# Batch 0's v loaded in two halves of heads, the second among the first weight slices, and the opening's scores, transposes and values in another order

## Chip, cores and metric

One core of a Trainium2 chip. The metric is the device time of one execution in microseconds; a profile's span, which is shown too, is some 2 us shorter. The four runs of the kernel before lie within 0.88 us, 0.24%. Times of "the kernel before" beside an experiment come from the same chip and rounds.

## The reference

Causal attention over 8 batches of 8 heads, with 16 beacon keys that every query sees, followed by a gated feed-forward block over all 4,608 tokens:

```python
B, H, S, Nb, D = 8, 8, 576, 16, 64
k_all = concat([beacon_k, k], axis=2); v_all = concat([beacon_v, v], axis=2)
scores = q @ k_all.T / sqrt(D)            # causal mask on the 576 own keys
attn = softmax(scores) @ v_all            # (B, H, S, D)
x = attn.transpose(0, 2, 1, 3).reshape(B * S, H * D)        # (4608, 512)
out = (gelu(x @ w_gate) * (x @ w_val)) @ w_out              # d_ff = 1536
```

Inputs and outputs are float32 in HBM; the kernel computes in bf16, and the loads convert.

## The kernel before

Heads are worked in four pairs (`m`). `transpose_both(0, m)` turns q and k of a pair on TensorE. `scores(0, (m, c))`, here `c((m, c))`, computes one of four chunks of a pair's scores and its exponential. `av` multiplies a pair's exponentials with v and normalises; `av_head` does one head. `turn` and `put` transpose the result into the feed-forward's input. Batch 0 has nothing to overlap with: it is the opening, and the dense gate/value matmuls (`gv_mms`) begin at its end.

```python
psum_s = ctx.enter_context(tc.tile_pool(name="psum_s", bufs=3, space=bass.MemoryType.PSUM))
psum_t = ctx.enter_context(tc.tile_pool(name="psum_t", bufs=1, space=bass.MemoryType.PSUM))
psum_o = ctx.enter_context(tc.tile_pool(name="psum_o", bufs=1, space=bass.MemoryType.PSUM))
# ... cut
def key_loads(src, beacon, dst, b):        # five loads, one for each tile of up to 128 keys
    parts = [(dst[NB:P, 0, :, :], src[b, :, 0:112, :].rearrange("h p d -> p h d"))]
    # ... cut: beacon
    for j in range(1, 5):
        n = KROWS[j]
        r0 = 112 + (j - 1) * P
        parts.append((dst[0:n, j, :, :], src[b, :, r0 : r0 + n, :].rearrange("h p d -> p h d")))
    return [lambda o=o, i=i: dma(o, i) for o, i in parts]      # dma: issued by GpSimd
# ... cut
def attend(b, m, hi, x_ps):                # 15 matmuls of one head
    expT, v_sb = exp_ring[:, m, :, :], v_ring[b % NRING]
    for j in range(5):
        for t in range(j + 1):
            e0 = EXP_OFF[t] + (j - t) * P
            mm(x_ps[:, j * DV : (j + 1) * DV], expT[0 : KROWS[t], hi, e0 : e0 + P],
               v_sb[0 : KROWS[t], t, 2 * m + hi, 0:DV], t == 0, t == j, skip_group_check=True)
# ... cut: the loads of the opening; load_qk6(b, h0, h1) loads k, then q of heads h0 to h1
load_qk6(0, 2, 4, (0,))
load_qk6(0, 4, 6)
load_qk6(0, 6, H)
for load in key_loads(v, beacon_v, v_ring[0][:, :, :, 0:D], 0)[1:]:
    load()
load_gate_val(0, 2)
load_gate_val(2, 4)
load_gate_val(4, 8)
# ... cut: the compute, see the diff
turn(0, 0); put(0, 0, by_act=True)
turn(0, 1, psum_o, "o"); put(0, 1, by_act=True)
av(0, 3)
gv_mms(0, 0, 0)
turn(0, 2); put(0, 2, by_act=True)
gv_mms(0, 1, 0)
turn(0, 3, psum_o, "o"); put(0, 3)
```

The softmax here doesn't subtract the row's maximum and nothing guards it: scores larger than these inputs give would overflow.

## Time and profile before

| | before |
|---|---|
| median of 4 runs | 366.34 us (365.75 to 366.63) |
| span of the profile, mean granted clock | 364.4 us, 0.999 |
| TensorE busy | 354.3 us, 97% |
| last y transposes of batch 0 end, dense stretch begins | 24.02 us |
| last load of v lands / last of four 256 KB weight slices lands | 16.34 / 21.62 us |

The first 24 us are the only place that the change touches; most of the page is shown in the prediction. One more view belongs here, the waits of TensorE from 7 to 34 us (who waited for whom: total, times, longest):

```profile
PE s_ps L168 <- DVE qkT L217: 1.3, 3, 0.5
PE s_ps L168 <- ACT qkT L171: 0.7, 1, 0.7
PE t_ps L176 <- DMA qk<-in_q_dram: 0.6, 1, 0.6
PE s_ps L168 <- issue: 0.2, 1, 0.2
```

In sum 2.8 us, in pieces of at most 0.7: this is what a better order could win, and it also tells that TensorE never stood for long.

### The profile page before, as it was taken

How to read it: one execution, taken by the hardware profiler on the slowest of the kernel's cores; microseconds unless marked ns; L12 is line 12 of the kernel's file. 1: busy time of each engine (PE TensorE's matmuls, PEld its weight loads, DVE VectorE, ACT ScalarE, POOL GpSimd, SP SyncE). 2: the span in 40 equal slices, each digit the busy share in tenths (PEclk: the TensorE clock that was granted, in tenths of full speed). 3: DMA queues.
4: the chain of work that ended last, by engine and by line, in shares of the span. 5: the costliest groups of instructions: out<-in, count | busy, mean ns of one | idle time of the engine just before them, and what ended most of it. 6: DMA issues, size and time to landing. Idle time of an engine off the chain costs nothing.

```text
span 364.4 us, 7627 instructions
## 1 busy us (share of the span) xinstructions
PE 354.3 (97%) x3127; PEld 184.6 (51%) x3170; DVE 155.4 (43%) x305; ACT 189.0 (52%) x243; POOL 161.2 (44%) x288
## 2 busy tenths in 40 slices
PE   7899999999999999999999999999999999999996
PEld 6664446444654456445644464446544564444443
DVE  4546545433454335343533354434444353333332
ACT  3973489136933594339723892379335953321210
POOL 8934388565537452954475554646330530000000
PEclk9999999999999999999999999999999999999999
DMA  7999999799069995999299927991697033000103
GB/s 103 175 203 204 197 124 91 125 187 186 20 121 126 199 87 65 171 216 64 57 146 208 126 35 120 178 197 24 108 142 132 17 64 114 0 0 31 58 34 112
DMA packets 160419, 41.57 MB, mean 114 GB/s; under 512 B 146944, under 2 KB 155904, under 8 KB 160384
## 3 DMA queue, kind: packets, MB, share of 16 engines
q0 software_dynamic: 104848, 19.11, 69.5%
q1 hardware_dynamic: 55536, 21.96, 29.3%
q8 instruction: 25, 0.41, 0.5%
q14 instruction: 10, 0.08, 0.1%
HBM read 38.27 MB, written 9.44 MB: 131 GB/s over the span
## 4 chain that ended last, share of the span: by engine, by line
PE 94%; issue 1%; DMA 1%; DVE 1%; POOL 1%; POOLq 0%; DVEq 0%
PE gv_ps L168 48%; PE o_ps L168 25%; PE x_ps L168 9%; PE s_ps L168 8%; PE v_ps L168 2%; PE g_ps L168 2%; DMA qk<-in_q_dram 1%; PE t_ps L176 1%; DVE qkT L213 1%; POOL qk L111 0%; PE y_ps L176 0%; DVE hT_sb L426 0%; POOL eye L480 0%; DVE o_sb L445 0%; DVE qkT L217 0%
## 5 line engine op out<-in xcount | busy, mean ns | idle before, releaser
L171 ACT ACTIVATE ge_sb<-gv_ps 128x512 bf16<-128x512 f32 x101 | 59.4, 597 | 142.8 <-PE gv_ps L168 140.6
L426 DVE TENSOR_TENSOR hT_sb<-gv_ps,ge_sb 128x512 bf16<-128x512 f32 x101 | 69.0, 691 | 113.5 <-ACT ge_sb L171 111.1
L168 PE MATMUL gv_ps<-xT_sb,wg_sb 128*128 128x512 bf16 x402 | 111.4, 379 | 0.5
L168 PE MATMUL gv_ps<-xT_sb,wv_sb 128*128 128x512 bf16 x388 | 107.9, 379 | 0.4
L171 ACT ACTIVATE expT<-s_ps 128x992 bf16<-128x992 f32 (+3 forms) x112 | 100.6, 974 | 6.5 <-PE s_ps L168 5.4
L168 PE MATMUL o_ps<-wo_sb,hT_sb 128*128 128x512 bf16 (+2 forms) x420 | 99.9, 373 | 2.0 <-issue 0.9
L298 POOL TENSOR_SCALAR_AFFINE_SELECT expT<-expT 128x256 bf16<-128x256 bf16 (+1 forms) x140 | 52.3, 390 | 52.9 <-ACT expT L171 51.8
L168 PEld LDWEIGHTS <-wv_sb 128*128 128x128 bf16 x432 | 42.3, 98 | 50.6
L168 PEld LDWEIGHTS <-wg_sb 128*128 128x128 bf16 x432 | 42.0, 98 | 50.0
L168 PEld LDWEIGHTS <-hT_sb 128*128 128x128 bf16 x444 | 39.9, 98 | 41.7 <-issue 1.7
L168 PEld LDWEIGHTS <-expT 128*128 128x128 bf16 (+1 forms) x960 | 33.6, 97 | 9.8 <-DVE y_sb L334 2.9
L445 DVE COPY o_sb<-o_ps 128x512 f32<-128x512 f32 (+2 forms) x37 | 24.9, 672 | 31.2 <-PE o_ps L168 30.2
L168 PE MATMUL x_ps<-v_sb,expT 128*128 128x65 bf16 (+1 forms) x960 | 37.4, 193 | 0.0
L111 POOL DMA_DIRECT2D v_sb<-in_v_dram x40 | 33.6, 857 | 5.9 <-DMA wv_sb<-in_moe_w_val_dram 1.7
L168 PE MATMUL s_ps<-qkT 64*128 64x80 bf16 (+5 forms) x528 | 33.1, 250 | 2.3 <-DVE qkT L217 1.3
L111 POOL DMA_DIRECT2D k_sb<-in_k_dram x30 | 25.2, 842 | 14.7 <-DMA q_sb<-in_q_dram 11.3
L334 DVE TENSOR_TENSOR y_sb<-x_ps,r_sb 128x320 bf16<-128x320 f32 (+1 forms) x47 | 28.8, 612 | 1.6
L111 POOL DMA_DIRECT2D q_sb<-in_q_dram x30 | 25.3, 874 | 5.2 <-DMA wo_sb<-in_moe_w_out_dram 3.6
L332 DVE RECIPROCAL r_sb<-x_ps 128x5 f32<-128x5 f32 (+1 forms) x47 | 9.6, 204 | 42.3 <-PE x_ps L168 42.3
L168 PEld LDWEIGHTS <-qkT 64*128 64x128 bf16 x528 | 17.1, 95 | 17.8 <-issue 12.9
L377 POOL COPY hold_sb<-xT_sb 128x2 bf16<-128x2 bf16 x6 | 1.1, 186 | 31.1 <-DMA xT_sb<-y_sb 31.1
L111 POOL DMA_DIRECT2D k_sb<-in_beacon_k_dram x6 | 3.2, 534 | 13.4 <-DMA v_sb<-in_v_dram 13.4
(54 smaller groups left out, 123.3 us busy)
## 6 DMA issues: line engine op xcount, KB each, us to landing
out_dram<-o_sb SPq DMA_DIRECT2D x35, 256.0 KB, 7.0
v_sb<-in_v_dram POOLq DMA_DIRECT2D x24, 128.0 KB, 9.1
q_sb<-in_q_dram POOLq DMA_DIRECT2D x18, 128.0 KB, 11.8
k_sb<-in_k_dram POOLq DMA_DIRECT2D x18, 128.0 KB, 5.9
wo_sb<-in_moe_w_out_dram POOLq DMA_DIRECT2D x3, 512.0 KB, 14.4
wg_sb<-in_moe_w_gate_dram POOLq DMA_DIRECT2D x2, 512.0 KB, 11.4
wv_sb<-in_moe_w_val_dram POOLq DMA_DIRECT2D x2, 512.0 KB, 13.0
v_sb<-in_v_dram POOLq DMA_DIRECT2D x8, 112.0 KB, 5.4
```

The lines of the kernel that those rows point to most:

```text
L111: keep(nc.gpsimd.dma_start(out=out_ap, in_=in_ap))
L168: keep(nc.tensor.matmul(out_ap, lhsT, rhs, start=start, stop=stop, **kw))
L171: keep(nc.scalar.activation(out_ap, in_ap, func, **kw))
L176: keep(nc.tensor.transpose(out_ap, in_ap, ident[0:n, 0:n]))
L213: keep(nc.vector.tensor_copy(out_ap, in_ap))
L298: nc.gpsimd.affine_select(out=d, in_=d, pattern=[[0, 2], [1, n]], compare_op=ALU.is_ge, fill=0.0, base=0, channel_multiplier=-1,)
L332: keep(nc.vector.reciprocal(r, x[:, :, :, D:DV]))
L334: nc.vector.tensor_tensor(out=y_of[i][:, :, h0:h1, :].rearrange("p j b d -> p b j d"), in0=x[:, :, :, 0:D], in1=r.to_broadcast([P, h1 - h0 ...
L377: keep(nc.gpsimd.tensor_copy(hold_sb, x[:, 0 : S : S - 1]))
L426: nc.vector.tensor_tensor(out=h_of[ci][:, fi, :], in0=gv_of.pop((ci, fi))[1], in1=ge_sb, op=ALU.mult)
L445: keep(nc.vector.tensor_copy(o_sb[:, ti, c0:c1], o_ps))
```

## The change

Its intent: v of heads 0 to 3 arrives before q and k of the last pair, so that the first pair's values can fill TensorE's idle time. They now stand right behind chunk (2,1), the heads of pairs 1 and 2 stand singly between the last chunks, and the transposes of pairs 1 and 3 come one chunk later. The other half of v shares the queue with the weights that the gate/value matmuls want. The diff in full:

```diff
--- before.py
+++ after.py
@@ -153,9 +153,13 @@
         for load in key_loads(v, beacon_v, v_ring[b % NRING][:, :, :, 0:D], b):
             load()
 
-    def load_gate_val(f0, f1):
+    def v_half(h0):
+        hs = slice(h0, h0 + 4)
+        return key_loads(v[:, hs], None, v_ring[0][:, :, hs, 0:D], 0)
+
+    def load_gate_val(f0, f1, ws=(0, 1)):
         fs = slice(f0 * P, f1 * P)
-        for w in range(2):
+        for w in ws:
             dma(
                 (wg_sb, wv_sb)[w][:, :, fs],
                 (moe_w_gate, moe_w_val)[w][:, fs].rearrange("(kk p) f -> p kk f", p=P),
@@ -489,11 +493,14 @@
     )
     load_qk6(0, 2, 4, (0,))
     load_qk6(0, 4, 6)
+    for load in v_half(0):
+        load()
     load_qk6(0, 6, H)
-    for load in key_loads(v, beacon_v, v_ring[0][:, :, :, 0:D], 0)[1:]:
+    first = [lambda f0=f0, w=w: load_gate_val(f0, f0 + 2, (w,)) for f0 in (0, 2) for w in (0, 1)]
+    for load in v_half(4):
         load()
-    load_gate_val(0, 2)
-    load_gate_val(2, 4)
+        if first:
+            first.pop(0)()
     load_gate_val(4, 8)
     load_qk6(1, 0, 4)
     load_kb(1)
@@ -521,25 +528,26 @@
     transpose_both(0, 0)
     c((0, 0))
     c((0, 2))
+    c((0, 1))
     transpose_both(0, 1)
-    c((0, 1))
     c((1, 0))
     c((1, 2))
     transpose_both(0, 2)
     c((0, 3), (1, 3))
     c((1, 1))
     c((2, 0))
+    c((2, 2))
     transpose_both(0, 3)
-    c((2, 2))
     c((2, 1))
+    av(0, 0)
     c((3, 0))
+    av_head(0, 1, 0, psum_t, "t")
+    c((2, 3), (3, 3))
+    av_head(0, 1, 1, psum_o, "o")
     c((3, 2))
-    av_head(0, 0, 0, psum_t, "t")
-    av_head(0, 0, 1, psum_o, "o")
-    c((2, 3), (3, 3))
-    av(0, 1)
+    av_head(0, 2, 0, psum_t, "t")
     c((3, 1))
-    av(0, 2)
+    av_head(0, 2, 1, psum_o, "o")
     turn(0, 0)
     put(0, 0, by_act=True)
     turn(0, 1, psum_o, "o")
```

## The prediction

> **What bounds the kernel now.** I read the page first, then the chain of waits up to 30 us, then the engines one by one in the first 30 us, and last the DMA issues in short windows.
>
> ```profile
> PE 354.3 (97%) x3127; PEld 184.6 (51%) x3170; DVE 155.4 (43%) x305; ACT 189.0 (52%) x243; POOL 161.2 (44%) x288
> PE 94%; issue 1%; DMA 1%; DVE 1%; POOL 1%; POOLq 0%; DVEq 0%
> ```
>
> TensorE is busy for 354.3 of 364.4 us and makes up 94% of the chain that ended last. After the opening there is no wait of note on it, so whatever moves the start of the dense gate/value matmuls of chunk 0 moves the end by as much. The change touches only what lies before them. In the record before, the last of batch 0's four y transposes begins at 23.75 us and the dense stretch at 24.02 us: I take 24.02 as the mark.
>
> ```profile
> 14.21 1.42 DVE qkT L213 x2
> 15.63 0.08 DVE qkT L217
> 15.72 0.05 issue
> 15.76 0.90 PE s_ps L168 x12
> 16.66 1.02 PE x_ps L168 x30
> ...
> 23.27 0.43 PE gv_ps L168 x2
> 23.71 0.05 issue
> 23.75 0.43 PE y_ps L176 x5
> ```
>
> This is the chain in order of time (start, length, what). Up to 15.76 it hops between transposes and their copies; from 15.76 to 24 it is TensorE in program order, with a pause of 0.20 at 19.43 ("issue") and about 0.2 ahead of the last transposes. Beside it ScalarE does the exponentials:
>
> ```profile
> 9.96 9.59 ACT L171 ACTIVATE expT<-s_ps 128x992 bf16<-128x992 f32 x11 [0.46 <-PE s_ps L168]
> 20.16 1.00 ACT L171 ACTIVATE expT<-s_ps 128x992 bf16<-128x992 f32 x1 [0.60 <-PE s_ps L168]
> ```
>
> Eleven in a row without a gap, 9.59 / 11 = 0.87 us each, a gap of 0.46 before them and of 0.60 before the last. These two gaps and TensorE's idle time before 15.76 are what the reordering aims at. Now the loads:
>
> ```profile
> 7.00 4.20 POOL L111 DMA_DIRECT2D v_sb<-in_v_dram  x5
> 15.95 0.68 POOL L111 DMA_DIRECT2D qk<-in_k_dram  x1 [0.24 <-DMA v_sb<-in_v_dram]
> 19.59 0.76 POOL L111 DMA_DIRECT2D wg_sb<-in_moe_w_gate_dram  x1 [1.65 <-DMA wv_sb<-in_moe_w_val_dram]
> v_sb<-in_v_dram POOLq DMA_DIRECT2D x1, 80.0 KB, 5.9
> wv_sb<-in_moe_w_val_dram POOLq DMA_DIRECT2D x1, 256.0 KB, 8.3
> kb<-in_beacon_k_dram POOLq DMA_DIRECT2D x1, 16.0 KB, 12.4
> 12.00:14.00 2.00, 1.60 (x45) 1.17 (x45) 1.15 (x3) 2.00 (x3) 2.00 (x3) 1.00 2.42 154
> 18.00:20.00 2.00, 1.80 (x50) 1.43 (x44) 1.35 (x4) 1.55 (x2) 0.41 (x1) 1.00 1.45 195
> ```
>
> Three lines are issues, three are issues with their time to landing, two are windows with DMA share and GB/s at the end. Issue start plus time to landing: the last tile of v is issued at 10.35 and lands at 16.25, just ahead of the first values matmul (16.59); the last of the four small weight slices is issued at 13.36 and lands at 21.66. Sixteen KB of beacon keys need 12.4 us, so the loads queue behind one another and size hardly matters. v moves at 154 GB/s, the weights at 195 to 207. From about 3 us the DMA engines never rest here: the transfers are the limit, not the issuing.
>
> [...] landings follow issue order, and the 12.4 us of the beacon keys are the wait for what stood ahead. [...] The trace has the clock at 1.00 throughout, with pauses of 0.7 us at most[...].
>
> **The change part by part.**
>
> *Loads.* Five loads of v (576 KB) become ten of half the heads. Bytes are the same. An issue of a full tile takes about 0.85 us, that of the 80-row one 0.77, of the 16 KB beacon 0.53: as an estimate from these, 0.65 for a half. The order becomes q and k up to the third pair, first half of v (288 KB), q and k of the fourth pair, then half tile, gate slice, half tile, value slice, and so on, the fifth half tile last. In the trace before, q of the third pair lands at 5.13 + 5.5 = 10.6 us and from there the queue drains continuously:
> - first half of v: 288 KB (0.295 MB) at 154 GB/s = 1.9, lands by 12.5;
> - q and k of the fourth pair: 288 KB in the 1.6 us of before (10.6 to 12.2) or a little more, 14.2 (before 12.2);
> - second half of v, 1.9, and four slices of 256 KB (1.05 MB) at 200 GB/s, 5.2: together 7.1, so the last half tile lands near 21.4; the half tiles one by one near 14.6, 16.4, 18.0, 19.7, 21.4.
>
> The sum is a cross-check: the same bytes ended at 21.66 before, with a weight slice last. Issuing: ten times 0.65, six of 0.63 and 0.80 put the last half tile's issue end near 17, so it isn't what is late. (Some issues also start about 0.3 us after the landing of the load eight places earlier: 15.95 after 15.6, 19.59 after 19.3. With that the estimate is still 17.)
>
> *Scores and transposes up to 16 us.* The third chunk of pair 0 no longer sits behind the transposes that wait for q until 8.96; ScalarE runs three exponentials from 7.65 to 10.4 and pauses 0.4 for the keys of pair 1, as before 0.46. Gain about 0.1, for eleven exponentials then follow at 0.87 from 10.8. The fourth pair's transposes come at 13.9 and finish when q lands, 14.75; their copies (1.42 + 0.16) end at 15.85. Before: 15.71. The chunk of pair 3 isn't needed before 16.1, so this delay is hidden.
>
> *First values pair.* It runs at 15.15 to 16.2, as soon as the exponential of chunk (2,0) frees its PSUM tile, in what was idle time; all it reads landed at 12.5. That takes 1 us out of the stretch after 15.76. With everything on time I follow: (3,0) 16.2, half of pair 1 16.55, (2,3)+(3,3) 17.1, other half 17.5, (3,2) 18.0, first head of pair 2 at 18.4.
>
> *The new wait.* That head is head 4, in the second half of v. Its fifteen matmuls (0.51 us) go through the key tiles; the last five need the fifth half tile, 21.4. So TensorE stands in parts from about 18.7 to 21.45, and, since it runs in program order, chunk (3,1) stands behind it. From there:
> - last matmuls to 21.7, chunk (3,1) 0.4 to 22.1, its exponential 22.2 to 23.15;
> - other head of pair 2 to 22.6, its normalisation 0.7 to 23.4 (it holds the tile that the turn of pair 1 wants), turn of pair 0 beside it, turn of pair 1 at 23.45 to 23.7;
> - values of pair 3, 0.95, 24.65; gate/value 0.43, turn 0.26, gate/value 0.43 give 25.8;
> - normalisation of pair 3 (0.22 + 0.82) is ready at 25.75; last turn 0.27: dense start near 26.05.
>
> Against 24.02 that is 2.0 us later. Without the new wait the same walk gives (3,1) at 18.9 to 19.3, and, with the turn of pair 1 waiting 0.4 for its tile, a dense start near 23.4 to 23.7: 0.3 to 0.6 earlier. So reordering +0.4 gain, loads −2.4 net of it.
>
> **The rivals.**
> 1. *v is in time after all*: 365.9. For it: [...] the author will have wanted it. Against: order in the queue, and 1 MB of weights that must pass first. It would have to come 2 us sooner.
> 2. *GpSimd's issuing becomes the bound*: if a half costs as much as a full tile, five more issues add at most 5 x 0.85 = 4.2 us up to the last small slice: 14.2 + 4.2 = 18.4, still before 21.4. Time as in the main case. Later weights (slices of features 4 to 8) landed at 24.2 and 26.7 before and are first read at 30.07, a slack of 3 us; the shift of the dense start widens it.
> 3. *The clock falls in the stall*: two pauses of about 1.0 and 1.5 us, broken by five matmuls[...].
> 4. *The stall is absorbed later*: TensorE shows only 0.05 us pauses in the chain from 24 to 45 us, so there is nothing to absorb it.
>
> **Range and chances.** 366.33 + 2.0, less a little because I may have put the last half tile too late (at 20.9 the loss is 1.5), makes 368.2. Rival 1 stretches the low end to about 366.3 and rival 3 with a late queue the high end to 369.3. Two per cent are 7.3 us, out of reach of anything found here; the verdict "same" is nearly sure.
>
> **What would show it.** Right: in the trace after, the values matmuls of head 4 idle before a DMA of v for over 1 us in all between 18 and 22; the last half tile lands at 20.8 to 21.8; the exponential of (3,1) starts after 21.5 (20.16 before); the first values matmul is at about 15.2; the dense start is at 25.5 to 26.2. Wrong: head 4 runs without a wait, or the last v lands before 19; then the time falls to about 366. If the loss is there but the values wait for nothing, another wait has taken its place and my reading of the loads failed.

Rival 3 was priced near 370 us. The forecast's sum came to a dense start near 26.05, 2.0 us after 24.02, and to 366.33 + 2.0, less a little, so 368.2 us. The high end of the range, 369.3, leaned on rival 3; it was the author's estimate. Two exceptions to "1.00 throughout" and "0.7 us at most": the trace of before has a clock of 0.50 in the last 0.6 us of its span, after TensorE's work, and a pause of 1.1 us ahead of the first warm-up matmul.

## The result

The changed kernel takes **371.81 us** (371.50 to 372.86, 4 runs) against 366.34 us. A ratio here is the mean time of one kernel's fast runs over that of the other's of the same rounds, so not quite the ratio of these medians: 1.0156, interval 1.0131 to 1.0181. That is 1.6% slower; the prediction had 368.2, with a range of 366.3 to 369.3. Span 370.2 us.

The page's busy time of TensorE and the clock in 40 slices of 9.3 us, changed kernel:

```profile
PE 360.6 (97%) x3170; PEld 187.4 (51%) x3170; DVE 155.6 (42%) x307; ACT 189.5 (51%) x243; POOL 164.2 (44%) x293
...
PEclk9869999999999999999999999999999999999999
```

The second and third slices have a lower clock (0.8 and 0.6 in whole tenths). TensorE is even busier than before (354.3): at the lower clock matmuls were busy for longer (thirty values matmuls 1.65 us against 1.02, below), so busy time hides this loss. The chain of work that ended last, 16 to 34 us, changed kernel (start, length, what):

```profile
17.08 6.19 DMA v_sb<-in_v_dram
23.27 0.04 issue
23.31 0.22 PE x_ps L172
23.53 0.81 PE s_ps L172 x9
24.33 0.95 PE x_ps L172 x15
...
26.09 0.67 PE y_ps L180 x5
26.76 1.65 PE x_ps L172 x30
```

The chain no longer starts from a transpose's copy but from the last half tile of v, issued at 17.08 and landed at 23.27 (before 17.08, outside this view, it runs through GpSimd's issues from 11.23 on). Behind it come, in program order, one matmul of head 4, the chunk (3,1) and the rest. Thirty values matmuls take 1.65 us; in the chain of before they took 1.02. The dense stretch begins at 29.99 us, 5.97 after the 24.02 of before; the span grew by 5.8. All of the loss is in the opening.

TensorE's longest wait from 7 to 34 us, and stretches with TensorE's busy time (second pair of numbers: us busy, instructions) and, third from the end, the granted clock:

```profile
PE x_ps L172 <- DMA v_sb<-in_v_dram: 3.1, 2, 1.8
...
12.00:15.30 3.30, 3.30 (x57) 2.36 (x55) 1.15 (x4) 3.30 (x5) 3.30 (x5) 0.50 1.27 143
...
18.80:22.20 3.40, 1.37 (x30) 0.95 (x27) 0.74 (x3) 1.58 (x2) 2.65 (x5) 1.00 1.55 175
22.40:28.90 6.50, 5.27 (x72) 4.28 (x72) 1.78 (x6) 2.30 (x3) 2.46 (x5) 0.50 1.26 203
```

The clock fell twice, to 0.50: from 11.93 to 15.34 us and from 22.17 to 29.00 us, by the clock records of the trace. The second fall lies exactly on the path from v's landing to the dense stretch. The GpSimd queue shows how the loads were issued (start, us, what; in brackets the idle time before):

```profile
5.75 3.62 POOL L111 DMA_DIRECT2D v_sb<-in_v_dram  x5
...
11.23 0.72 POOL L111 DMA_DIRECT2D v_sb<-in_v_dram  x1 [0.61 <-DMA qk<-in_q_dram]
...
17.08 0.71 POOL L111 DMA_DIRECT2D v_sb<-in_v_dram  x1
```

A half tile costs 0.72 us to issue on average over the five, hardly less than the 0.84 of a full one.

### The profile page after: what moved, and what is told of

Same layout as the page of the kernel before. It is cut to its first block, busy times and chain, and to the rows that moved or that the text cites. A ratio compares the mean times of both kernels' runs of the same rounds, so it can differ in the third digit from the quotient of the medians.

```text
span 370.2 us, 7677 instructions
## 1 busy us (share of the span) xinstructions
PE 360.6 (97%) x3170; PEld 187.4 (51%) x3170; DVE 155.6 (42%) x307; ACT 189.5 (51%) x243; POOL 164.2 (44%) x293
## 4 chain that ended last, share of the span: by engine, by line
PE 93%; DMA 3%; POOL 2%; issue 0%; DVE 0%; POOLq 0%
PE gv_ps L172 47%; PE o_ps L172 26%; PE x_ps L172 8%; PE s_ps L172 7%; DMA v_sb<-in_v_dram 2%; PE v_ps L172 2%; PE g_ps L172 2%; DMA qk<-in_q_dram 2%; PE t_ps L180 1%; POOL v_sb L111 1%; POOL qk L111 1%; POOL wg_sb L111 0%; POOL wv_sb L111 0%; PE y_ps L180 0%; DVE y_sb L338 0%
## 5 line engine op out<-in xcount | busy, mean ns | idle before, releaser
L172 PE MATMUL gv_ps<-xT_sb,wv_sb 128*128 128x512 bf16 x404 | 111.7, 379 | 0.0
L172 PE MATMUL o_ps<-wo_sb,hT_sb 128*128 128x512 bf16 (+2 forms) x444 | 104.7, 373 | 0.0
L172 PE MATMUL x_ps<-v_sb,expT 128*128 128x65 bf16 (+1 forms) x960 | 39.3, 196 | 3.2 <-DMA v_sb<-in_v_dram 3.1
L172 PEld LDWEIGHTS <-expT 128*128 128x128 bf16 (+1 forms) x960 | 34.9, 99 | 11.9 <-issue 3.4
L111 POOL DMA_DIRECT2D v_sb<-in_v_dram x45 | 36.8, 834 | 7.0 <-DMA wv_sb<-in_moe_w_val_dram 1.9
L172 PE MATMUL s_ps<-qkT 64*128 64x80 bf16 (+6 forms) x528 | 33.8, 255 | 1.8 <-DVE qkT L221 1.0
L172 PEld LDWEIGHTS <-qkT 64*128 64x128 bf16 x528 | 17.2, 96 | 18.5 <-issue 14.2
```

The source lines that it names most:

```text
L111: keep(nc.gpsimd.dma_start(out=out_ap, in_=in_ap))
L172: keep(nc.tensor.matmul(out_ap, lhsT, rhs, start=start, stop=stop, **kw))
```

## The experiments

My theory after the result: the loads did it, through a v that lands at 23.3 instead of 21.4 us and through the clock that falls in the wait. Rivals: the new order itself; the clock as a mere symptom. Eleven runs of ten different kernels follow. Some of their diffs are abridged, and the labels are not quite in order.

### e1: the new order with the old loads

```diff
 # changed kernel with the loads of before
-    for load in v_half(0): load()
     load_qk6(0, 6, H)
-    # second half one by one with the weight slices
+    for load in key_loads(v, beacon_v, v_ring[0][:, :, :, 0:D], 0)[1:]: load()
+    load_gate_val(0, 2); load_gate_val(2, 4)
```

> The new order of the compute with the old loads. My theory (the loss of 5.5 us comes from the loads: v's second half lands at 23.3 us behind 1 MB of weights, and the tensor clock falls while TensorE waits for it): no wait for v beyond about 16.3 us, no fall of the clock after 20 us, dense gate/value stretch near 24.2 us, time 366.5 (365.8 to 367.2). The first fall of the clock (12 to 15.3 us) should still be there if the third chunk of pair 0 ahead of the transposes causes it. Rival (the order itself is the loss: a head of pair 2 ahead of the last chunk, and single PSUM tiles that make turn wait for normalisation): 369 or more.

Measured: 367.07 us, ratio 1.0027 (1.0012 to 1.0042); dense stretch at 24.75 us in its profile; clock 0.995 to 1.0 in five runs. No wait for v is shown. TensorE's waits, 7 to 34 us as before:

```profile
PE s_ps L172 <- DVE qkT L221: 1.5, 2, 1.1
PE s_ps L172 <- ACT qkT L175: 0.7, 1, 0.7
PE y_ps L180 <- DVE y_sb L338: 0.6, 1, 0.6
```

They sum to 2.8 us again. The 0.6 for q and the 0.5s for keys became one piece of 1.1, and the turn of pair 1 now waits for the normalisation that holds its PSUM tile. So the order isn't the loss of 5.5 us, but it isn't a gain either: it costs about 1 us where I had credited 0.4. The first fall of the clock, which I had expected in this run, wasn't there in the profile.

### e2: the new loads with the old order

```diff
 # before's sequence of transpose_both, c, av, av_head; the changed kernel's loads
```

> The new loads with the old order of the compute. My theory: v's last half tile lands near 23.3 us as in the changed kernel; the values of pair 2 wait for it, but the last chunk and its exponential are done by then, so the dense stretch begins at 26.5 us if the clock holds and near 28.5 if it falls: 368.8 to 370.8. No fall of the clock at 12 us, since the third chunk of pair 0 stands behind the transposes again. Rival (the order is the loss): 366 to 367.

Measured: 370.23 us, ratio 1.0114 (1.0098 to 1.0130), as the theory said. Values of pair 2 wait 2.7 us for v, the last half tile's matmul starts at 23.27, the clock is at half from about 24.2 to 27.6 us (means of 0.54 and 0.60 over 24 to 26 and 26 to 28), dense stretch at 28.17. The rival is out: the loads alone give 4.2 us of the loss. Loads and order added (4.2 + 1.0) are about the whole (5.7 by the ratio).

### e3: both halves of v ahead of the weights

```diff
-    first = [lambda f0=f0, w=w: load_gate_val(f0, f0 + 2, (w,)) for f0 in (0, 2) for w in (0, 1)]
     for load in v_half(4):
         load()
-        if first:
-            first.pop(0)()
+    load_gate_val(0, 2)
+    load_gate_val(2, 4)
```

> As the changed kernel, but the five loads of v's second half stand together ahead of the weight slices. My theory: they land by 16.5 us, head 4 waits for nothing, the last small slice lands near 21.5 (22.95 in the changed kernel), dense stretch near 24.0 us, time 366.2 (365.6 to 367.0). If the interleaving itself costs DMA time (half tiles between slices took 0.8 us each instead of 0.4), the 4 slices and 5 half tiles here take 7.1 us and not 9.0. Rival (ten small loads are slow wherever they stand): last slice at 23 us, values late, 368 or more.

Measured: 368.06 us, ratio 1.0068 (1.0044 to 1.0093), 367.5 to 370.3, with the higher times in the runs of lower clock (0.991, 370.3; 1.0, 367.5). Head 4 waits for nothing, as expected. But the other expectations missed, the time (365.6 to 367.0) among them: v's last load landed near 17.6 us, and the last small slice at 16.58 + 7.9 = 24.5 us, later still than in the changed kernel. And the span grew by 2.0 us although the dense stretch began at 24.98, only 0.96 later than before. The rest is lost just before 55.5 us: TensorE waits 1.2 us for a causal mask on GpSimd. e10 takes up both points.

### e4: the wait filled with dummy matmuls

```diff
     for j in range(5):
+        for _ in range(fill[j]):     # (0, 0, 0, 50, 40), head 4 only
+            mm(x_ps[:, 384:448], idle[:, 0:P], idle[:, 0:D], True, True, skip_group_check=True)
         for t in range(j + 1):
```

> The changed kernel with 50 and 40 matmuls of zeros (64 columns, into unused columns of the same PSUM tile) ahead of the last two key tiles of head 4, that is in the wait for v. My theory: v still lands at 23.3 us, but the clock stays at 1.00 after 20 us, and the work from there to the dense stretch takes about 4.7 us (6.7 in the changed kernel): dense stretch near 28.0, time 369.8 (369.3 to 370.4), so 1.6 to 2.2 us below the changed kernel. Rival (the clock is a symptom and costs nothing on the path): 371.5 to 372.

Measured: 373.13 us, ratio 1.0185 (1.0164 to 1.0207): no gain over the changed kernel, its median even 1.3 us higher. The clock was still full near 26.7 us (five y transposes from 26.33 on took 0.42 us, as in the kernel before; 0.67 at half clock in the changed one), but with the added instructions came a wait of another kind. TensorE in order of time, and the instruction queue from 23.8 to 26.3 us:

```profile
26.23 0.27 PE L172 MATMUL x_ps<-v_sb,expT 128*128 128x65 bf16 x3 [1.82 <-issue]
```

```profile
q8 instruction: 1, 0.02, 2.4%
```

In the middle of a head TensorE stood 1.82 us for no data, while one block of instructions came in. That the block was what it stood for is not shown: such a block comes in near this time in other kernels too (at 22.15 us in the changed one) without a wait of this kind. The test of the clock is void; it was made again with the number of instructions unchanged.

### e6: the wait filled, the number of instructions kept

```diff
-    warm(66)      # 64 columns each
+    warm(33)      # 128 columns each
+        # ahead of key tiles 3 and 4 of head 4: 18 and 15 matmuls of zeros
+        mm(x_ps[:, 328:512], idle[:, 0:P], idle[:, 0:184], True, True, skip_group_check=True)
```

> The filling of the wait once more, this time with 18 and 15 matmuls of zeros of 184 columns, and with 33 warm-up matmuls of 128 columns in place of 66 of 64, so that TensorE has as many instructions as in the changed kernel. In the first try the clock held up to 27 us [...]. Theory (the clock's fall costs about 2 us of the path): [...] the clock stays at 1.00 from 16 us on, v lands near 23.2, dense stretch near 28.0, time 369.8 (369.3 to 370.4). [...] Rival (the clock costs nothing on the path): 371.5 or more [...].

Measured: 370.23 us, ratio 1.0115 (1.0095 to 1.0134), against 1.0156 of the changed kernel. The same two stretches in this kernel:

```profile
18.80:22.20 3.40, 2.86 (x51) 2.54 (x48) 0.86 (x3) 1.71 (x2) 2.26 (x5) 1.00 1.61 179
22.40:28.90 6.50, 5.87 (x103) 4.37 (x101) 2.80 (x7) 3.47 (x5) 2.61 (x4) 1.00 1.27 205
```

The clock stays at 1.00, and v's last matmuls still end near 23.6 us. The dense stretch begins at 28.31 us instead of 29.99. So useless work, put where TensorE waits anyway, wins back about 1.5 us of time: the second fall of the clock is a cause on the path. The late v and the order are the rest: with the clock held the time is still 4.2 us above the kernel before. The first fall (12.04 to 15.45 us) was in this run too, so it isn't what costs.

### e5: the last chunk ahead of head 4

```diff
     c((3, 2))
+    c((3, 1))
     av_head(0, 2, 0, psum_t, "t")
-    c((3, 1))
```

> The changed kernel with chunk (3,1) put ahead of head 4, so that it no longer stands behind the wait for v. Theory (program order behind the late v costs the chunk's own time, some 0.8 us at half clock; the rest of the loss is v and the clock): dense stretch near 29.2 us, time 371.0 (370.5 to 371.4), 0.5 to 1.0 below the changed kernel. Rival (the chunk and its exponential behind the wait are the main part): 369.5 or less. [...]

Measured: 371.61 us, ratio 1.0152 (1.0135 to 1.0169): the gain that I expected is barely there. Dense stretch at 29.63. There was no first fall of the clock in this profile (1.00 from 8 to 22 us), and that changed nothing either. Program order behind the late v is a small term; v and the second fall stay.

### e7: the weight slices ahead of v's second half

```diff
     load_qk6(0, 6, H)
+    load_gate_val(0, 2)
+    load_gate_val(2, 4)
     for load in v_half(4):
         load()
-        if first:
-            first.pop(0)()
```

> As the changed kernel, with the four weight slices ahead of the five loads of v's second half. Theory (the changed kernel's DMA queue runs low between 10 and 15 us, because half tiles of 64 KB are issued at 0.72 us each, 91 GB/s, and GpSimd waits 0.6 us for a landing; large slices issued first keep it full): the last half tile lands at 21.3 to 21.9 and not at 23.3, although it stands last here too; dense stretch 26.5 if the clock holds, up to 28.3 if it falls, time 368.6 to 370.6. Rival (v's second half is slow to move wherever it stands): lands at 23 or later, time 371.5 or more.

Measured: 371.43 us, ratio 1.0151. The last half tile landed at 17.4 + 5.6 = 23.0 us. This expectation failed: large loads in front didn't make the nine loads quicker (23.27 in the changed kernel). Either mixing or the small loads themselves had to be the cause, which the next two runs separate. This trace already tells something, in two windows (GB/s at the end of the line):

```profile
13.00:14.00 1.00, 0.61 (x14) 0.35 (x10) 0.41 (x2) 1.00 (x3) 1.00 (x3) 1.00 0.51 61
20.00:21.00 1.00, 0.00 (x0) 0.00 (x0) 0.00 (x0) 0.05 (x1) 0.75 (x1) 1.00 2.26 154
```

The queue had already run low at 13 to 14 us, behind the first five half tiles: the first slice was issued only at 11.57 us, after GpSimd had stood 0.95 us for the landing of a q. The second five half tiles, with a full queue ahead of them, then moved at 154 GB/s, as full tiles did before. So half tiles were not slow to move here; what they did is let the queue run low.

### e9 and e11: full tiles mixed with weight slices

```diff
 # order of compute: before
     load_qk6(0, 6, H)
-    for load in key_loads(v, beacon_v, v_ring[0][:, :, :, 0:D], 0)[1:]: load()
-    load_gate_val(0, 2); load_gate_val(2, 4)
+    # tile 0 of v (all heads), gate slice, tile 1, value slice, tile 2, gate slice, ...
```

> Old order of the compute; the five full tiles of v stand behind q and k of the fourth pair, one by one with the four weight slices. It asks why the loads of the changed kernel moved only 2.89 MB by 22 us (3.28 MB before). If mixing v with weights slows the queue, the DMA rate between 13 and 20 us is near 150 GB/s here too and about 2.9 MB are moved by 22 us; if the small loads of half the heads are the cause, it is near 185 and 3.2 MB or more. Either way the first values wait for the last tile at 21.4 to 23 us, so the time is long: 370 to 373.

Three runs took 372.4 us, one 939 us, and the profile was of that one, with TensorE's weight loads waiting for "issue" throughout (574 us in all); why, I don't know. It is left out of the ratio (1.0173). The kernel was run again for a profile:

> The kernel of the full tiles mixed with weight slices, once more and for its profile alone, because the profile of the first time fell into a run of 939 us. Expected if full tiles mixed with weights don't slow the queue, as that profile's first 22 us say: 3.2 to 3.3 MB moved by 22 us, v's last tile at 21.3 us, values of pair 0 waiting for it, 372.4 us. If the slow state falsified those first 22 us: about 2.9 MB and v's last tile at 23.

It took 372.54 us (one run, so of unknown state), and v's last tile landed at 22.2 us. The stretch from 14 to 22 us, GB/s at the end of the line, of the kernel before, the changed one and this one:

```profile
14.00:22.00 8.00, 7.34 (x192) 6.13 (x189) 4.61 (x11) 7.11 (x10) 5.12 (x9) 1.00 1.50 196
```

```profile
14.00:22.00 8.00, 6.17 (x143) 4.89 (x140) 3.82 (x9) 5.93 (x7) 7.25 (x12) 0.92 1.47 158
```

```profile
14.00:22.00 8.00, 3.12 (x61) 2.09 (x60) 1.50 (x3) 4.74 (x6) 5.27 (x9) 0.82 1.71 187
```

Adding up 1 us windows from 2 us on, the kernel before had moved 3.28 MB by 22 us, this one 3.26 MB, the changed one 2.89 MB. Mixing full tiles with weights cost nothing in rate here. (Its values, which now need all of v, wait for it 4.7 us; hence the long time.)

### e10: half tiles where the full ones stood

```diff
 # kernel before, order of compute and of loads unchanged
     load_qk6(0, 6, H)
-    for load in key_loads(v, beacon_v, v_ring[0][:, :, :, 0:D], 0)[1:]:
-        load()
+    for pair in zip(v_half(0), v_half(4)):
+        for load in pair: load()
```

> Old order of the compute and old order of the loads, but each of the five loads of v in two halves of four heads, one behind the other. If small loads are the cause of the lost DMA rate (GpSimd issues one in 0.72 us, so 64 KB come at 91 GB/s), v's last load lands at 17.4 to 18 us (16.25 before), 3.0 MB or less are moved by 22 us, and the values of pair 0 wait about 1 us: 366.8 to 367.6. If mixing is the cause, v lands by 16.8, 3.2 MB or more by 22 us, and the time is 366.0 to 366.6.

Measured: 369.21 us, ratio 1.0074 (1.0054 to 1.0094), 2.79 MB by 22 us. Windows from 14 to 17 us, before and in this kernel:

```profile
14.00:17.00 3.00, 2.54 (x62) 1.81 (x59) 1.50 (x3) 3.00 (x5) 2.70 (x5) 1.00 1.71 186
```

```profile
14.00:17.00 3.00, 2.54 (x68) 1.94 (x65) 1.40 (x5) 3.00 (x4) 3.00 (x5) 1.00 1.27 88
```

The small loads are the cause of the lost rate: ten issues of 0.72 us bring at most 64 KB each, 91 GB/s, less than the queue drains (154 for v); the time from issue to landing shrinks from 5.3 to 2.7 us from the first half tile to the last, a queue running empty, and the rate drops to 88 GB/s. v itself landed at 16.3 us, in time; my figure of 17.4 missed, since the last issues meet an empty queue. Where are the 2.7 us lost then? TensorE's waits from 48 to 60 us:

```profile
PE x_ps L172 <- POOL expT L302: 1.8, 2, 1.7
```

The late weights hold GpSimd: its later loads wait for landings, the last four loads of q for batch 2 are issued from 48.4 us (45.8 before), and the causal masks of batch 1 stand behind them in its program. In that wait the clock falls again (mean 0.61 from 56 to 60 us). It is the 1.2 us of e3. The changed kernel shows no such wait; there TensorE comes to batch 1 some 6 us later.

A caution on marks from single profiles: the dense stretch of this run began at 22.82 us, 1.2 earlier than in the profile of the kernel before, with the same order of compute. The q of the second pair had landed at 8.20 us instead of 8.96 (e8: 8.01, dense stretch at 23.32). So such marks differ by about a microsecond through one early load alone; the ratios over several runs are the firmer evidence.

### e8: an attempt at a better kernel

```diff
 # kernel before
     c((2, 3), (3, 3))
-    av(0, 1)
     c((3, 1))
+    av(0, 1)
     av(0, 2)
```

> The kernel before, loads and order, with only the chunk (3,1) ahead of the values of pair 1. It is meant as a version better than both: ScalarE's gap of 0.6 us before the last exponential should close. Expected: last exponential starts at 19.6 us (20.16 before), dense stretch near 23.7 us (24.02), time 365.9 (365.6 to 366.3), 0.3 below the kernel before. Rival (TensorE in program order is the limit there, so that nothing is won): 366.1 to 366.4.

Measured: 365.98 us against 366.03 of the kernel before, ratio 1.0000 (0.9985 to 1.0015). ScalarE's gap is closed (before: 11 exponentials in a row, then a gap of 0.60):

```profile
7.50 12.38 ACT L171 ACTIVATE expT<-s_ps 128x1024 bf16<-128x1024 f32 x14 [0.56 <-PE s_ps L168]
```

but nothing is won that five rounds can show. No version beat the kernel before.

## Why the prediction was wrong

The direction and the wait that causes the loss were right, the size was not: +2.0 us predicted, +5.5 measured. Two steps failed, by about as much each: the landing of v's last half tile, and the clock. The prediction's terms, with what the runs showed:

- **The new wait: right.** Head 4 waits for v, 3.1 us in two pieces, with chunk (3,1) behind it, whose exponential starts at 24.38 us (20.16 before; "after 21.5" predicted); e2 shows that the loads alone bring most of the loss.
- **"Second half of v ... together 7.1, so the last half tile lands near 21.4": too small by 1.9 us.** It landed at 23.27. Up to q and k of the last pair the estimate held (14.2; measured 9.94 + 4.3 = 14.2). From there the nine loads took 9.1 us. How much is left without the clock's fall e6 shows: 370.23 us, 4.2 above the kernel before, about 1 of them the order's. I had put a half tile's issue at 0.65 us by a line through other sizes and concluded that transfers stay the limit. It is 0.72 on average for 40 to 64 KB, against 0.84 for the full tiles of 80 to 128 KB and 0.53 for the 16 KB of beacon keys: halving a load saved 0.12 us of 0.84, and it took away the lead of the issues over the queue (88 GB/s instead of 186 in the same 3 us, e10). e10 and e11 show that it is the small loads and not the mixing. What stays open: also after 17 us, with a queue of 6 us ahead, the changed kernel moved only 143 to 184 GB/s until 22; issuing alone doesn't explain that. (A small misreading in the same place: the last full tile of v was issued at 10.43 us and landed at 16.34, not 10.35 and 16.25; nothing hangs on it.)
- **Rival 3, the clock, dismissed: this is the other step that failed.** I had taken two pauses of about 1.0 and 1.5 us for too short; that was my estimate, on no trace of this case. They were 1.80 and 1.34 us, and the clock fell to 0.50, for 6.8 us. In the 3.4 us up to the fall (18.8 to 22.2) TensorE was busy for 1.37 us; with 2.86 in the same stretch of e6 the clock held. At how little work it falls the runs don't tell: from 8.55 to 11.95 us TensorE was busy for 2.25 us in the changed kernel, where the clock fell at 11.93, and for 2.26 in e1, where it held. Nor do they tell why its changes lie where they do (11.93, 15.34, 22.17 and 29.00: 3.41, 6.83 and 6.83 us apart). From the landing of v to the dense stretch my walk had 4.65 us (21.4 to 26.05); at half clock it took 6.7, in e6 at full clock 4.9 (23.4 to 28.3). The term is 1.5 us by the times of e6 and the changed kernel, 1.8 to 2.1 by these marks.
- **"Reordering +0.4 gain": wrong.** e1 has the order at 1 us slower. The first values pair does run at about 16 us (15.2 predicted), but the waits elsewhere grew by as much, above all the turn of pair 1 for its PSUM tile. The changed kernel is 1.6 us slower than e2, which has the same loads. How much of that is the order itself stays open, for the clock was at half for 6.8 us on the path there and for 3.4 in e2.
- **"GpSimd's issuing becomes the bound": dismissed too soon.** It didn't bound the last half tile directly (17.8 at the end of its issue, near my 17), but it let the queue run low before (102 GB/s from 13 to 14 us, 154 in the kernel before). GpSimd's later loads also started about 0.3 us after the landing of the load eight places earlier (11.23 after 10.95 in the changed kernel; 19.59 after 19.30 before). Whether that is the chip or the way this program is built, no run shows.
- **Slack later on: right for the changed kernel,** whose chain has no new wait after 30 us; e3 and e10 show that without the stall the late loads would have bitten at 53 to 56 us.

Together: 26.05 + 1.9 (v) + 2.0 (clock) = 29.95, measured 29.99. This sum is bookkeeping and no check: its last term is what the stretch from v's landing to the dense stretch took beyond my 4.65 us. The check is e6, which took 4.9 there at full clock.

## What to carry to other kernels

A load split in two is issued twice, at 0.72 us for each half here where the whole took 0.84: before splitting, set bytes per issue time of the halves (here 64 KB in 0.72 us, 91 GB/s) against the rate at which the queue drains (here 154 GB/s), not only the bytes. When a change makes TensorE wait, look at the granted clock and at TensorE's busy time over the whole stretch and not only at the longest pause: here the clock fell to 0.50 with no pause over 1.80 us, after 3.4 us with 1.37 us busy. Price the wait together with the work behind it at the clock that the trace shows (6.7 us here for what took 4.9 at full clock); dummy matmuls in the wait tell quickly whether the clock is on the path, if the number of instructions is kept (with more of them, e4, another wait of 1.82 us came in). Look at what a late load does to its issuing engine long after: here masks 30 us later, for which TensorE waited 1.8 us (e10).
